# Splitting the 512-column matmuls of an expert layer's output product into two of 256 columns

## The chip, the cores and the metric

The kernel runs on one NeuronCore of a Trainium2 chip. The metric is the device time of one execution in microseconds (us). Durations of single instructions are given in nanoseconds (ns).

## The reference

Three layers follow one another; the change lies in the third. The tokens are N = 2304, the model width is 512.

```python
# 1. attention with keys and values averaged over groups of 8 (4 batches, 8 heads, 576 x 64)
# 2. gated layer: (sigmoid(x @ w_gate) * (x @ w_val)) @ w_out, width 1536
# 3. eight experts, width 1024 each, all of them for every token:
P = np.exp(logits - logits.max())              # logits = x @ w_gate, [N, 8]
for _ in range(8):                             # rows and columns normalised in turn
    P /= P.sum(1, keepdims=True) + 1e-09
    P /= P.sum(0, keepdims=True) + 1e-09
    P *= N / E
for e in range(E):
    h = np.maximum(x @ w1[e], 0.0)             # first product
    ye = h @ w2[e]                             # second product: the one that is changed
    out += P[:, e:e+1] * ye
```

## The kernel before, in words

All large products take fp32 data split into a high and a low part of the type fp32r, and multiply in three passes (high with high, high with low, low with high: `PASSES`, L260). Every `nc.tensor.matmul` becomes two instructions on TensorE: a weight load (LDWEIGHTS, the `lhsT` operand, 128 rows by up to 128 columns) and a MATMUL, which streams the columns of `rhs` past those weights into a bank of PSUM. The trace keeps the loads on a row of their own (PEld). Consecutive matmuls never share a load, even where they use the same `lhsT` (the first two passes do).

The attention and the gated layer take the first third of the time. Their large products are made by `mm` (L262, matmuls at L268) and `x2_step` (L506, matmuls at L560), all with 384 streamed columns. Attention has small matmuls of plain fp32, such as the scores at L351 (64 rows of weights, 72 columns).

The expert layer works through 96 steps (`steps2`: 3 pairs of token blocks, 8 experts, 4 parts of the expert's width; the loop begins at L973). A pair holds two blocks of 384 tokens. In each step:

- The first product is made by seven block products (`product`, L895, matmuls at L903), six matmuls of 384 columns each, with sums and differences of blocks as operands (prepared by GpSimd and ScalarE in `prep_w1`, L697 to L708). Their results go through ScalarE copies (L1011, L1019, L1026), VectorE additions (L1032, L1038, L1045) and `hidden` (L913), which applies the ReLU and splits the result into the tiles `h`, two buffers each.
- The second product of the step before is made by `y_chunk` (L922), called six times, once for every 128 tokens. Each call takes a bank of 512 fp32 from the tag "big" (four buffers), runs six matmuls of 512 columns into it (two halves of the width `fh`, three passes each; `lhsT` is a 128-column slice of `h`, `rhs` a row of `w2hl`, the split weights of `prep_w2`, L716 and L717), and hands the bank to VectorE, which multiplies by the token's share `prob` and adds to `acc` in one instruction (L963).

The order of TensorE's work is the order in which the loop writes it: a product, then a `y_chunk`, and so on, so that the engines that finish a product have the following six matmuls' time for it. After the last step six calls of `y_chunk` follow with nothing between them (L1057), and the results leave by DMA from `acc` (L967). The change touches only the six matmuls of `y_chunk`, L929 to L937: 3456 matmuls in all (96 steps, 6 calls, 6 each).

Of the kernel before, what the change touches and what calls it, by code (L numbers as in the profile page):

```python
# [20 lines left out]
def attention_moe_moe_kernel(  # L21
# [31 lines left out]
    nc = tc.nc  # L53
    NT, DM = out.shape
# [30 lines left out]
    def bank(tag, bufs):  # L85
        return ps.tile([128, 512], F32, tag=tag, name=tag, bufs=bufs)
# [173 lines left out]
    PASSES = ((0, 0), (0, 1), (1, 0))  # L260
# [406 lines left out]
    raw1, raw2, wsum, w2hl = {}, {}, {}, {}  # L667
# [59 lines left out]
    with tc.manual_schedule():  # L727
# [151 lines left out]
        hs = {}  # L879
# [42 lines left out]
        def y_chunk(n, t):  # L922

            if n < 0:
                return
            p, e, q = steps2[n]
            half, i = divmod(t, TPB)
            cs = slice(i * 128, (i + 1) * 128)
            py = bank("big", 4)  # L929
            m = 0  # L930
            for fh in range(2):
                h = hs[n, fh, half]
                for s, o in PASSES:
                    nc.tensor.matmul(  # L934
                        out=py, lhsT=h[:, s, cs], rhs=w2hl[n][:, o, fh], start=(m == 0), stop=(m == 5)
                    )
                    m += 1  # L937
            tt = p * CPP + t
            pr = prob[:, tt, e : e + 1]
            if p == 0 and e < LATE:  # L940
                if q == 0:
                    raw_acc[e, t] = pools["more"].tile([128, DM], F32, tag="acc", name="acc", bufs=LATE * CPP)
                    nc.scalar.copy(out=raw_acc[e, t], in_=py)
                else:
                    nc.vector.tensor_tensor(out=raw_acc[e, t], in0=py, in1=raw_acc[e, t], op=ALU.add)
                return
            if e == 0 and q == 0:
                acc[t] = pools["more"].tile([128, DM], F32, tag="acc", name="acc", bufs=LATE * CPP)
                nc.vector.tensor_scalar_mul(out=acc[t], in0=py, scalar1=pr)
            else:  # L950
                if p == 0 and t not in acc:
                    acc[t] = raw_acc[0, t]
                    nc.scalar.activation(out=acc[t], in_=acc[t], func=AF.Copy, scale=prob[:, tt, 0:1])
                    for i in range(1, LATE):
                        nc.vector.scalar_tensor_tensor(
                            out=acc[t],
                            in0=raw_acc[i, t],
                            scalar=prob[:, tt, i : i + 1],
                            in1=acc[t],
                            op0=ALU.mult,  # L960
                            op1=ALU.add,
                        )
                nc.vector.scalar_tensor_tensor(  # L963
                    out=acc[t], in0=py, scalar=pr, in1=acc[t], op0=ALU.mult, op1=ALU.add
                )
            if (e, q) == (E - 1, QF - 1):
                nc.sync.dma_start(out=out[tt * 128 : (tt + 1) * 128], in_=acc[t])  # L967
# [5 lines left out]
        for n, (p, e, q) in enumerate(steps2):  # L973
# [38 lines left out]
            if last_of_pair:  # L1012
                load_xf(p + 1, 0)
            y_chunk(n - 1, 3)
            slot2()
            if n > 0:
# [3 lines left out]
            if last_of_pair:  # L1020
                load_xf(p + 1, 3)
            y_chunk(n - 1, 4)
            slot2()
            product(n, "P6", pa, False)
            c2 = c_tile()
            nc.scalar.copy(out=c2, in_=pa[:, :TB])  # L1026
            if last_of_pair:
                load_xf(p + 1, 4)
            y_chunk(n - 1, 5)
            slot2()  # L1030
            product(n, "P3", pc, False)
# [86 lines left out]
```

## Time and profile before

| What | Value |
|---|---|
| Time, median of 2 runs | 2180.82 us (2176.22 and 2185.43) |
| Span of the profiled execution, first to last instruction | 2185.2 us |
| The run's time that stands beside that span | 2185.43 us |
| TensorE matmul, busy | 2096.2 us (96%), 10973 instructions |
| TensorE weight load, busy | 1905.0 us (87%), 10973 instructions |
| VectorE, ScalarE, GpSimd, busy | 65%, 40%, 41% |
| Matmuls of the changed line, L934 | 3456, recorded 394 ns each |

The span belongs to one execution; the run nearest to it took 0.2 us more. A matmul's record is longer than the time until the next matmul starts, because matmuls follow one another in a pipeline and the recorded end is modelled. The distance from one start to the next ("pitch" below) therefore tells more than the recorded length. The records of weight loads likewise may overlap one another.

### The profile page before, as it was taken

To read this page: it belongs to the slowest core of one execution; us is meant where nothing else is said; L and a number is where in the kernel's file an instruction comes from. 1 tells how busy PE (TensorE), PEld (TensorE's weight loads), DVE (VectorE), ACT (ScalarE), POOL (GpSimd) and SP (SyncE) were. 2 spreads that over 40 slices of the span, in tenths; PEclk is the share of its full clock that TensorE was granted. 3 is DMA by queue.
4 is the path that set the end of the run, shared out by engine and by line. 5 is a ranking of instruction groups with operands and counts; after the bars stand their busy time and mean duration, and the time that the engine had idled before them with its cause. 6 is when DMAs were issued, how large, how long until landed. Compare 5 with 4: busy or idle time off the path is not lost.

```text
span 2185.2 us, 28656 instructions
## 1 busy us (share of the span) xinstructions
PE 2096.2 (96%) x10973; PEld 1905.0 (87%) x10973; DVE 1422.6 (65%) x2172; ACT 882.5 (40%) x1607; POOL 891.5 (41%) x780
## 2 busy tenths in 40 slices
PE   4679999999999999999999999999999999999999
PEld 4568989988997888888888898989888888898988
DVE  6846876644435877666666666666666666666665
ACT  4334343454544444434343434343433343434342
POOL 1100000353554465454545454545454545454541
PEclk8679999999999999999999999999999999999999
DMA  7432553453562132121215121212125212121211
GB/s 227 143 119 85 167 171 116 131 181 106 194 228 92 59 116 78 61 75 60 76 59 206 58 78 58 78 58 78 58 78 188 77 58 78 58 78 58 78 58 39
DMA packets 87451, 222.09 MB, mean 102 GB/s; under 512 B 8849, under 2 KB 8849, under 8 KB 87313
## 3 DMA queue, kind: packets, MB, share of 16 engines
q1 hardware_dynamic: 82128, 210.81, 28.5%
q10 hardware_dynamic: 5184, 9.44, 1.2%
q8 instruction: 86, 1.41, 0.3%
q14 instruction: 53, 0.43, 0.1%
HBM read 189.55 MB, written 30.67 MB: 101 GB/s over the span
## 4 chain that ended last, share of the span: by engine, by line
PE 86%; DVE 6%; issue 3%; ACT 2%; DMA 1%; POOL 1%; SPq 0%; ACTq 0%; DVEq 0%; POOLq 0%
PE big L934 37%; PE at L903 18%; PE gv L903 14%; PE gv L268 10%; PE big L560 4%; DVE wa_lo L236 1%; PE at L351 1%; DMA narrow<-made 1%; PE at L437 1%; DVE made L166 1%; DVE made L165 1%; DVE g L821 1%; ACT wa_hi L231 1%; PE at L422 0%; DVE wide L175 0%
## 5 line engine op out<-in xcount | busy, mean ns | idle before, releaser
L934 PE MATMUL big<-w2hl,h 128*128 128x512 f32 x3456 | 893.8, 394 | 0.0
L934 PEld LDWEIGHTS big<-w2hl,h 128*128 128x128 f32 x3456 | 642.0, 188 | 102.2
L963 DVE SCALAR_TENSOR_TENSOR acc<-big,prob,acc 128x512 f32<-128x512 f32 x516 | 385.6, 748 | 264.8 <-PE big L934 258.7
L705 POOL TENSOR_TENSOR fa<-raw,fa 128x768 fp32r<-128x768 f32 x96 | 179.4, 1869 | 440.0 <-PE big L934 403.2
L268 PE MATMUL gv<-xs,wa_hi 128*128 128x384 f32 x1152 | 314.6, 355 | 20.9 <-ACT xs L447 8.1
L707 POOL TENSOR_TENSOR fs<-ss,fs 128x512 fp32r<-128x512 f32 x96 | 125.0, 1303 | 292.9 <-ACT fs L704 289.3
L268 PEld LDWEIGHTS gv<-xs,wa_hi 128*128 128x128 f32 x1152 | 217.1, 198 | 28.2 <-ACT xs L447 8.9
L917 ACT ACTIVATE h<-gv 128x384 fp32r<-128x384 f32 x192 | 94.3, 491 | 355.2 <-DVE gv L1045 196.4
L903 PE MATMUL at<-xf,fa 128*128 128x384 f32 x1152 | 233.7, 338 | 0.8 <-DVE c L1038 0.8
L903 PE MATMUL at<-xf,fs 128*128 128x384 f32 x1152 | 232.4, 337 | 0.4 <-ACT c L1011 0.4
L903 PE MATMUL gv<-xf,fs 128*128 128x384 f32 x1152 | 231.6, 336 | 0.0
L717 DVE TENSOR_TENSOR w2hl<-raw,w2hl 128x512 fp32r<-128x512 f32 x192 | 227.6, 1186 | 6.1 <-ACT w2hl L716 6.1
L903 PEld LDWEIGHTS at<-xf,fa 128*128 128x128 f32 x1152 | 206.6, 189 | 17.7 <-DVE c L1038 1.6
L903 PEld LDWEIGHTS gv<-xf,fs 128*128 128x128 f32 x1152 | 205.4, 188 | 16.3
L268 PE MATMUL gv<-xs,wa_lo 128*128 128x384 f32 x576 | 203.1, 353 | 14.8 <-DVE wa_lo L236 11.8
L903 PEld LDWEIGHTS at<-xf,fs 128*128 128x128 f32 x1152 | 204.4, 188 | 9.0 <-ACT c L1011 0.7
L918 DVE SCALAR_TENSOR_TENSOR h<-gv,h 128x384 fp32r<-128x384 f32 x192 | 107.2, 558 | 107.6 <-ACT h L917 107.6
L560 PE MATMUL big<-h,wa_hi 128*128 128x384 f32 x576 | 150.8, 343 | 0.0
L594 POOL TENSOR_TENSOR fx<-x,fx 128x768 fp32r<-128x768 f32 x10 | 18.4, 1844 | 316.5 <-DVE x L577 263.4
L236 POOL TENSOR_TENSOR wa_lo<-stage,wa_hi 128x512 fp32r<-128x512 f32 x67 | 99.6, 1499 | 81.3 <-ACT wa_hi L231 69.6
L268 PEld LDWEIGHTS gv<-xs,wa_lo 128*128 128x128 f32 x576 | 114.7, 199 | 17.7 <-DVE wa_lo L236 14.6
L708 POOL TENSOR_TENSOR fs<-ss,fs 128x512 fp32r<-128x512 f32 x96 | 125.5, 1307 | 0.0
(149 smaller groups left out, 2682.1 us busy)
## 6 DMA issues: line engine op xcount, KB each, us to landing
raw<-in_moe_w_dram SPq DMA_DIRECT2D x192, 512.0 KB, 3.8
stage<-narrow SPq DMA_DIRECT2D x150, 256.0 KB, 2.8
xd<-fx SPq DMA_DIRECT2D x21, 768.0 KB, 3.3
xf<-xd SPq DMA_DIRECT2D x21, 768.0 KB, 6.6
narrow<-made ACTq DMA_DIRECT2D x36, 256.0 KB, 2.0
wide<-in_moe_w_gate_dram SPq DMA_DIRECT2D x12, 512.0 KB, 3.8
wide<-in_moe_w_val_dram SPq DMA_DIRECT2D x12, 512.0 KB, 10.0
wide<-in_moe_w_out_dram SPq DMA_DIRECT2D x12, 512.0 KB
```

The lines of the kernel that those rows point to most:

```text
L236: eng.tensor_tensor(out=lo, in0=raw, in1=f32(hi), op=ALU.subtract)
L268: nc.tensor.matmul(out=out_, lhsT=a[s], rhs=b[m], start=(i == 0), stop=(i == n - 1))
L560: nc.tensor.matmul(out=x2p[d][:, :TB], lhsT=w[s][:, d * 128 : (d + 1) * 128], rhs=gs[j, f][m], start=(first and i == 0), stop=(last and i ...
L705: pl(out=fa[:, 1], in0=raw[:, 0:3], in1=f32(fa[:, 0]), op=ALU.subtract)
L707: pl(out=fs[:, 1, 0:2], in0=ss[:, 0:2], in1=f32(fs[:, 0, 0:2]), op=ALU.subtract)
L708: pl(out=fs[:, 1, 2:4], in0=ss[:, 2:4], in1=f32(fs[:, 0, 2:4]), op=ALU.subtract)
L717: nc.vector.tensor_sub(out=t[:, 1, i], in0=raw[:, i], in1=f32(t[:, 0, i]))
L903: nc.tensor.matmul(out=pt[:, :TB], lhsT=w[:, s, i, k], rhs=t[:, o, k], start=(start and m == 0), stop=(m == 5), skip_group_check=True,)
L917: nc.scalar.activation(out=t[:, 0], in_=src, func=AF.Relu)
L918: nc.vector.scalar_tensor_tensor(out=t[:, 1], in0=src, scalar=0.0, in1=f32(t[:, 0]), op0=ALU.max, op1=ALU.subtract)
L934: nc.tensor.matmul(out=py, lhsT=h[:, s, cs], rhs=w2hl[n][:, o, fh], start=(m == 0), stop=(m == 5))
L963: nc.vector.scalar_tensor_tensor(out=acc[t], in0=py, scalar=pr, in1=acc[t], op0=ALU.mult, op1=ALU.add)
```

## The change

In `y_chunk`, the six matmuls of 512 columns become two groups of six with 256 columns each: first all six for columns 0 to 255 of the bank, then all six for columns 256 to 511. Each of the twelve has a weight load of its own, so the same `lhsT` slice is loaded twice as often. The bank, its buffers and what follows on VectorE stay as they are.

```diff
             py = bank("big", 4)
-            m = 0
-            for fh in range(2):
-                h = hs[n, fh, half]
-                for s, o in PASSES:
-                    nc.tensor.matmul(
-                        out=py, lhsT=h[:, s, cs], rhs=w2hl[n][:, o, fh], start=(m == 0), stop=(m == 5)
-                    )
-                    m += 1
+            for d0 in range(0, DM, 256):
+                m = 0
+                for fh in range(2):
+                    h = hs[n, fh, half]
+                    for s, o in PASSES:
+                        nc.tensor.matmul(
+                            out=py[:, d0 : d0 + 256],
+                            lhsT=h[:, s, cs],
+                            rhs=w2hl[n][:, o, fh, d0 : d0 + 256],
+                            start=(m == 0),
+                            stop=(m == 5),
+                        )
+                        m += 1
             tt = p * CPP + t
```

## Rows read from the trace of the kernel before

**Rows 1.** The page: busy time by engine, and the chain by line.

```profile
PE 2096.2 (96%) x10973; PEld 1905.0 (87%) x10973; DVE 1422.6 (65%) x2172; ACT 882.5 (40%) x1607; POOL 891.5 (41%) x780
...
PE big L934 37%; PE at L903 18%; PE gv L903 14%; PE gv L268 10%; PE big L560 4%; DVE wa_lo L236 1%; PE at L351 1%; DMA narrow<-made 1%; PE at L437 1%; DVE made L166 1%; DVE made L165 1%; DVE g L821 1%; ACT wa_hi L231 1%; PE at L422 0%; DVE wide L175 0%
```

**Rows 2.** Busy time by stretch (us): the expert layer, 682 to 2181.

```profile
682.00:2181.00 1499.00, 1498.18 (x7460) 1345.50 (x7458) 1015.18 (x1501) 599.64 (x1067) 721.62 (x658) 1.00 0.23 78
```

**Rows 3.** Waits of TensorE between 690 and 2181 us (total, times, longest).

```profile
PE at L903 <- DVE c L1038: 0.8, 1, 0.8
```

**Rows 4.** Groups of instructions, shapes apart: busy us, mean ns of one; idle before.

```profile
L934 PE MATMUL big<-w2hl,h 128*128 128x512 f32 x3456 | 893.8, 394 | 0.0
L934 PEld LDWEIGHTS big<-w2hl,h 128*128 128x128 f32 x3456 | 642.0, 188 | 102.2
...
L903 PEld LDWEIGHTS at<-xf,fa 128*128 128x128 f32 x1152 | 206.6, 189 | 17.7 <-DVE c L1038 1.6
```

**Rows 5.** Timeline of TensorE's matmuls from 1500 us: start, length of the run, count.

```profile
1500.65 1.55 PE L934 MATMUL big<-w2hl,h 128*128 128x512 f32 x6
1502.04 1.21 PE L903 MATMUL gv<-xf,fs 128*128 128x384 f32 x6
1503.09 1.55 PE L934 MATMUL big<-w2hl,h 128*128 128x512 f32 x6
1504.48 1.22 PE L903 MATMUL at<-xf,fs 128*128 128x384 f32 x6
1505.53 1.55 PE L934 MATMUL big<-w2hl,h 128*128 128x512 f32 x6
1506.92 1.21 PE L903 MATMUL gv<-xf,fs 128*128 128x384 f32 x6
1507.96 1.20 PE L903 MATMUL at<-xf,fs 128*128 128x384 f32 x6
1509.00 1.55 PE L934 MATMUL big<-w2hl,h 128*128 128x512 f32 x6
```

**Rows 6.** Timeline of the weight loads, same stretch.

```profile
1500.48 1.29 PEld L934 LDWEIGHTS big<-w2hl,h 128*128 128x128 f32 x6
1501.81 1.12 PEld L903 LDWEIGHTS gv<-xf,fs 128*128 128x128 f32 x6
```

**Rows 7.** Timeline of VectorE at the end, one instruction per `y_chunk`.

```profile
2177.29 0.75 DVE L963 SCALAR_TENSOR_TENSOR acc<-big,prob,acc 128x512 f32<-128x512 f32 x1 [0.61 <-PE big L934]
2178.65 0.75 DVE L963 SCALAR_TENSOR_TENSOR acc<-big,prob,acc 128x512 f32<-128x512 f32 x1 [0.61 <-PE big L934]
2180.01 0.75 DVE L963 SCALAR_TENSOR_TENSOR acc<-big,prob,acc 128x512 f32<-128x512 f32 x1 [0.61 <-PE big L934]
```

**Rows 8.** Timeline of the weight loads around the scores, from 262 us.

```profile
262.26 0.96 PEld L351 LDWEIGHTS at<-kp,qt 64*128 64x128 f32 x8 [0.25 <-PE gv L268]
263.30 0.30 PEld L560 LDWEIGHTS big<-h,wa_hi 128*128 128x128 f32 x2
```

**Rows 9.** Timeline of the matmuls around the scores, from 262 us.

```profile
263.30 0.62 PE L560 MATMUL big<-h,wa_hi 128*128 128x384 f32 x2
```

**Rows 10.** Timeline of matmuls with weights of 8 columns, from 366 us.

```profile
366.24 0.52 PE L268 MATMUL at<-fx,wg_hi 128*8 128x384 f32 x2
366.59 0.34 PE L268 MATMUL at<-fx,wg_lo 128*8 128x384 f32 x1
366.77 0.51 PE L268 MATMUL at<-fx,wg_hi 128*8 128x384 f32 x2
```

**Rows 11.** Busy time by stretch: 160.4 to 162 us, granted clock 0.50 (third figure from the end).

```profile
160.40:162.00 1.60, 1.60 (x6) 1.60 (x6) 0.00 (x0) 0.30 (x1) 0.00 (x0) 0.50 0.92 292
```

**Rows 12.** Timeline of the matmuls in that stretch.

```profile
160.83 0.84 PE L268 MATMUL gv<-xs,wa_hi 128*128 128x384 f32 x2
161.47 0.52 PE L268 MATMUL gv<-xs,wa_lo 128*128 128x384 f32 x1
161.79 0.84 PE L268 MATMUL gv<-xs,wa_hi 128*128 128x384 f32 x2
162.44 0.52 PE L268 MATMUL gv<-xs,wa_lo 128*128 128x384 f32 x1
```

**Rows 13.** The page: DMA queues (packets, MB, share); q8 carries 16 KB packets of instructions.

```profile
q8 instruction: 86, 1.41, 0.3%
```

## The prediction

> **What bounds the kernel now.** I read the page first. TensorE's matmuls are busy for 96% of the span, and the chain that ended last runs through them: 37% of it is the changed line L934 and 32% the products at L903 [rows 1]. The reader should distrust the 96%, since the ends of matmuls are modelled, and look for idle time instead. The view by stretches says that between 682 and 2181 us, the whole expert layer, TensorE was busy for 1498.18 of 1499.00 us at a granted clock of 1.00, which is the higher level, 2.4 GHz [rows 2]. The waits of that stretch have one row, 0.8 us [rows 3]. So this layer lasts exactly as long as its matmuls take one after another. No other engine and no transfer ends last anywhere in it. What the change is worth is therefore the number of matmuls times the change in the distance from start to start, their pitch.
>
> The recorded length is not that pitch: 394 ns is the mean record at L934 [rows 4]. The pitch comes from the timeline. A run of six L934 matmuls starts at 1500.65 and the next run at 1502.04: 1.39 us for six. Three such runs give 4.17 us for 18, **231.7 ns for 512 columns**. The three runs at L903 that follow them take 1.05, 1.05 and 1.04 us, 3.14 us for 18, **174.4 ns for 384 columns** [rows 5]. Check: 3456 x 231.7 ns = 800.8 us, which is the 37% of the chain.
>
> **The change part by part.** It removes 3456 matmuls of 512 columns and adds 6912 of 256 columns. Columns streamed, operands, banks and the work of VectorE stay the same. What is added is 3456 further pairs of weight load and matmul start. Two costs are unknown, because no fp32r matmul under 384 columns stands in this trace: the pitch of the 256-column matmul by its own columns, and the pitch that its weight load forces.
>
> *By its columns.* A straight line through the two pitches has a slope of (231.7 - 174.4)/128 = 0.448 ns per column and meets zero columns at 2.5 ns. At 256 columns it gives 117.1 ns, almost half of 231.7. By this reading two halves cost 234.2 ns, 2.5 ns more than the whole. A less friendly reading comes from runs of one kind only. At the very end `y_chunk` follows `y_chunk`, and VectorE's instruction for each starts every 1.36 us, so six matmuls of 512 columns take 1360 ns, 226.7 each [rows 7]. Where a product follows a product, six of 384 take 1.04 us, 173.3 each (from 1506.92 to 1507.96 and on to 1509.00 [rows 5]). That line has a slope of 53.4/128 = 0.417 and meets zero at 13 ns: a fixed charge for every matmul. It gives 120.0 ns at 256 columns. Against a fixed charge speaks the stretch at half clock (0.50, the lower level of 1.2 GHz [rows 11]): there five starts span 162.44 - 160.83 = 1.61 us for five matmuls, 322 ns for 384 columns, and 384/1.2 is 320, so next to nothing is charged [rows 12]. I take **118 ns**, between 117.1 and 120.0 and nearer to the line that uses the same stretch.
>
> *By its load.* Each load is recorded with 188 ns, at L934 as at L903 [rows 4]. That is more than 118, so the reader must see whether loads can follow one another faster than their records. They do. At L903 the matmuls start every 174 ns with a 188 ns load each. The scores show it better: eight loads of 128 columns stand in 0.96 us, (960 - 188)/7 = 110 ns from load to load, with matmuls of only 72 columns between them [rows 8]. The two loads of L560 that follow cover 0.30 us, so the second began 0.11 us after the first [rows 8]. These loads are fp32r, and 0.11 us is what a load holds its place for. Does a load hide beneath the matmul before it? The first two matmuls there cover 0.62 us; the second one's record being about 0.34 us (a row of [rows 10] has that length for 384 columns), it began 0.28 us after the first, which is 0.11 of unhidden load plus one pitch of 0.17 [rows 9]. All later ones run at 0.174, so each load is hidden. And loads of 8 columns give no faster stream: 366.24 to 366.77 is 0.53 us for three matmuls, 177 ns [rows 10]. The load costs nothing as long as it fits: 110 ns fit beneath 117 to 120, with 7 to 10 ns to spare. That is the thin point of this forecast. For the load term I take 0 ns; its bounds are -11.7 ns per old matmul (pitch falls to the load's 110: 2 x 110 - 231.7) and, with nothing hidden, 2 x 110 more than the columns cost.
>
> The Trainium skill bears on this cover. "TensorE: Matmul & The Clock Gate", Part 3, under what overlaps and what doesn't, says that a weight load overlaps matmuls in flight only if it is aimed at other row groups of the array. Here every load takes all 128 rows, so by that rule each half would cost 117 + 110 = 227 ns and the kernel 3456 x (454 - 231.7) = 768 us more. The trace disagrees: a load of 110 ns and 384 columns, 160 ns at 2.4 GHz, would need 270 ns one after another, and the row shows 174.
>
> *The rest.* TensorE gets 6912 more instructions, and one of the instruction queues, q8, brought 86 packets of 16 KB; 1.41 MB over TensorE's 21,946 instructions is 64 bytes each, so I take it for TensorE's queue [rows 1, 13]. Some 27 more will come, in the expert layer one every 17.5 us instead of 26 (255 instructions a packet, and 21,830 instead of 14,918 in 1499 us [rows 2]). Cost: nothing now, as TensorE waits once in 1491 us [rows 3]; if every added packet stalled it for the time that one takes (0.3% of 16 x 2185 us over 86: 1.2 us), 33 us. I take 0. VectorE waits for the last matmul of a chunk as before and holds the bank for 0.75 of 1.36 us [rows 7]; the banks come free as before.
>
> *Sum.* 3456 x (2 x 118 - 231.7) ns = 3456 x 4.3 ns = +14.9 us. On the profiled execution that is 2185.4 + 14.9 = 2200.3 us. Its time lies 4.6 us above the median of the two runs, so on the median's scale I predict 2180.8 + 14.9 = **2195.7 us**: 0.7% more, less than the 2% that a measurement of this kernel can tell from no change. Each ns of the new pitch is worth 6.9 us, and 2% is 43.6 us: the pitch would have to pass 122.3 ns to be slower, or fall under 109.4 to be faster.
>
> **The rivals.**
>
> *The weight load takes over (slower).* The load of a matmul begins only when the matmul before has started: the two load runs start at 1500.48 and 1501.81, each about 0.17 to 0.23 us ahead of their first matmul, that is with the start of the one before [rows 5, 6]. If the loop of load, hand-over and next start is longer than 118 ns, it sets the pitch. Its length lies between 110 [rows 8] and 174 (it fits into L903's pitch); it decides from 122.3. If it needed the whole record and a start, 190 ns, the price would be 3456 x (380 - 231.7) = +512 us, but L903 excludes that. At 174, the longest that the rows allow, it is 3456 x 116.3 = +402 us, 2583; at 140 it is +167 us. For it: the loads would be in their place 110 of 118 ns, which no fp32r stream here has had to stand; the nearest, L903, has 110 of 174. Against it: the scores hold 110 with loads alone.
>
> The Trainium skill has a rule that leads to this side: "Perfetto Trace Analysis", on identifying the most-contended engine, wants TensorE's headroom judged by the busy share of its weight loads. That share is 87% now; 3456 more of 188 ns (650 us) would make 2555 us in a span of 2185, so the time would have to grow by hundreds of us. The rows of the scores speak against it, where 188 ns records start 110 ns apart.
>
> *A fixed charge of 13 ns per matmul (no change that can be told).* The pitch is 120.0, the price 3456 x 8.3 = +29 us, 2209.5. For it the pure runs, against it the half clock.
>
> *The halves run faster than half.* If what slows the long streams (231.7 for 512 columns, where 512/2.4 is 213.3) is absent in short ones, the load alone bounds the pitch at 110: 3456 x -11.7 = -40 us, 2140. For it: 226.7 at the end shows that the pitch isn't rigid. Against it: nothing in the rows gets shorter than its share of columns.
>
> *The loads are shared, so nothing is added.* Consecutive matmuls with the same `lhsT` have a load each today (10973 and 10973 [rows 1]), so the change does what it says.
>
> **How the numbers follow.** Pitch of 114 to 122.3, the forecast with the fixed charge: 0.68 (0.50 and 0.18). Load takes over, above 122.3: 0.23. Faster halves, under 114: 0.09, of which about half falls under 109.4. So faster by over 2%: 0.05; within 2%: 0.72; slower: 0.23. The range begins at 2150 (pitch 111.4, nearly the load's 110) and ends at 2250 (pitch 125.9), which takes in the first part of the load rival; about 0.04 lies below and 0.15 above.
>
> **What would show it.** In the profile after, a chunk of twelve matmuls should take 1.40 to 1.44 us before the next product starts, L934's successors should stand with 6912 matmuls of about 280 ns record (394 less 256 columns of 0.448), L903 should keep its 1.04 to 1.05 us, and TensorE's waits in the layer should stay near nothing, with the granted clock at 1.00. If the load takes over, twelve take over 1.47 us. If all L934 chunks agree but gaps of a us or more appear every 17 us or so, it is the instruction queue. I am wrong if a chunk of twelve leaves 1.33 to 1.47 us.

## The result, and the profile after

The changed kernel takes **2210.58 us** (median; 2209.08 and 2212.08) against 2180.82 before: a ratio of 1.0133, with an interval of 1.0104 to 1.0161. That is 23 to 35 us more, slower by less than 2%, and the interval excludes no change. The prediction was 2195.7 us within 2150 to 2250.

The page of the kernel after begins with the busy times by engine; its part on DMA queues has the packets of instructions.

```profile
PE 2120.2 (96%) x14429; PEld 2078.1 (94%) x14429; DVE 1420.5 (64%) x2172; ACT 883.0 (40%) x1607; POOL 891.6 (40%) x780
...
q8 instruction: 113, 1.85, 0.4%
...
L935 PE MATMUL big<-w2hl,h 128*128 128x256 f32 x6912 | 918.1, 283 | 0.0
L935 PEld LDWEIGHTS big<-w2hl,h 128*128 128x128 f32 x6912 | 898.6, 191 | 0.0
```

Against [rows 1] and [rows 4]: 3456 more matmuls and as many more loads, so no load was shared. The other engines' busy times are those of before. The view by stretches shows the expert layer and, last in its row, the clock and the DMA share:

```profile
682.00:2203.00 1521.00, 1520.27 (x10902) 1519.92 (x10901) 1013.36 (x1501) 599.54 (x1066) 721.33 (x658) 1.00 0.22 77
```

As in [rows 2], matmuls fill the stretch at a clock of 1.00. What is new is the second figure: loads now fill it too (1519.92 of 1521.00 us; 1345.50 of 1499.00 before). The waits of TensorE in the layer are still one row:

```profile
PE at L903 <- DVE c L1043: 0.7, 1, 0.7
```

So the time has not gone into a wait. It is in the pitch, the distance from start to start. Timeline of the matmuls from 1500 us (start, length, count):

```profile
1500.42 1.59 PE L935 MATMUL big<-w2hl,h 128*128 128x256 f32 x12
1501.85 1.20 PE L903 MATMUL gv<-xf,fs 128*128 128x384 f32 x6
1502.89 1.21 PE L903 MATMUL at<-xf,fs 128*128 128x384 f32 x6
1503.94 1.59 PE L935 MATMUL big<-w2hl,h 128*128 128x256 f32 x12
1505.37 1.20 PE L903 MATMUL gv<-xf,fa 128*128 128x384 f32 x6
1506.41 1.59 PE L935 MATMUL big<-w2hl,h 128*128 128x256 f32 x12
1507.84 1.21 PE L903 MATMUL at<-xf,fa 128*128 128x384 f32 x6
1508.88 1.60 PE L935 MATMUL big<-w2hl,h 128*128 128x256 f32 x12
1510.32 1.21 PE L903 MATMUL at<-xf,fa 128*128 128x384 f32 x6
```

Four chunks of twelve take 1.43, 1.43, 1.43 and 1.44 us, 5.73 us for 48: **119.4 ns a half**. Over all 569 chunks that stand between products the mean is 1.435 us, 119.6 ns a half. A chunk was 1.39 us [rows 5]. The products at L903 keep their 1.04 to 1.05 us. Now the sum: 3456 x (2 x 119.4 - 231.7) = +24.5 us. The starts of the line's first and last matmul give the same: 682.1 to 2180.9 us before and 680.0 to 2203.1 after, 1498.8 and 1523.2 us when not rounded first, +24.4. This stretch is called the layer's time below. The profiled spans differ by 22.1, as the first two layers happened to take 2 us less in the second one.

Timeline of VectorE at the end of the kernel after, where chunk follows chunk:

```profile
2199.14 0.75 DVE L968 SCALAR_TENSOR_TENSOR acc<-big,prob,acc 128x512 f32<-128x512 f32 x1 [0.69 <-PE big L935]
2200.59 0.75 DVE L968 SCALAR_TENSOR_TENSOR acc<-big,prob,acc 128x512 f32<-128x512 f32 x1 [0.69 <-PE big L935]
2202.03 0.75 DVE L968 SCALAR_TENSOR_TENSOR acc<-big,prob,acc 128x512 f32<-128x512 f32 x1 [0.69 <-PE big L935]
2203.46 0.75 DVE L968 SCALAR_TENSOR_TENSOR acc<-big,prob,acc 128x512 f32<-128x512 f32 x1 [0.69 <-PE big L935]
```

4.32 us for three chunks, 1.44 each: 120.0 ns a half, against 226.7 for a whole matmul in the same place [rows 7]. In such a uniform stream the halves cost 13.3 ns more than the whole; between products, where the whole takes 231.7, they cost 7.1.

### The profile page after: what moved, and what is told of

It reads as the page before. It is cut to its first block, busy times and chain, and to the rows that moved or that the text cites. A ratio compares the mean times of both kernels' runs of the same rounds, so it can differ in the third digit from the quotient of the medians.

```text
span 2207.3 us, 35657 instructions
## 1 busy us (share of the span) xinstructions
PE 2120.2 (96%) x14429; PEld 2078.1 (94%) x14429; DVE 1420.5 (64%) x2172; ACT 883.0 (40%) x1607; POOL 891.6 (40%) x780
## 4 chain that ended last, share of the span: by engine, by line
PE 87%; DVE 6%; issue 2%; ACT 2%; DMA 2%; POOL 0%; SPq 0%; ACTq 0%; DVEq 0%; POOLq 0%
PE big L935 37%; PE at L903 18%; PE gv L903 14%; PE gv L268 10%; PE big L560 5%; DVE wa_lo L236 1%; PE at L351 1%; DMA narrow<-made 1%; PE at L437 1%; DVE made L166 1%; PE at L422 1%; DMA wide<-in_moe_w_gate_dram 1%; DVE wide L175 1%; DVE g L821 0%; ACT wa_hi L231 0%
## 5 line engine op out<-in xcount | busy, mean ns | idle before, releaser
L935 PE MATMUL big<-w2hl,h 128*128 128x256 f32 x6912 | 918.1, 283 | 0.0
L935 PEld LDWEIGHTS big<-w2hl,h 128*128 128x128 f32 x6912 | 898.6, 191 | 0.0
L903 PE MATMUL at<-xf,fa 128*128 128x384 f32 x1152 | 233.5, 337 | 0.7 <-DVE c L1043 0.7
L903 PE MATMUL gv<-xf,fs 128*128 128x384 f32 x1152 | 233.2, 337 | 0.0
L903 PE MATMUL at<-xf,fs 128*128 128x384 f32 x1152 | 232.1, 336 | 0.4 <-ACT c L1016 0.4
L717 DVE TENSOR_TENSOR w2hl<-raw,w2hl 128x512 fp32r<-128x512 f32 x192 | 223.1, 1163 | 6.4 <-ACT w2hl L716 6.4
L903 PEld LDWEIGHTS at<-xf,fs 128*128 128x128 f32 x1152 | 197.6, 188 | 0.8 <-ACT c L1016 0.7
L903 PEld LDWEIGHTS at<-xf,fa 128*128 128x128 f32 x1152 | 193.9, 189 | 0.9 <-DVE c L1043 0.9
L903 PEld LDWEIGHTS gv<-xf,fs 128*128 128x128 f32 x1152 | 194.0, 190 | 0.2 <-issue 0.2
```

Of the source, the lines that this page charges most:

```text
L717: nc.vector.tensor_sub(out=t[:, 1, i], in0=raw[:, i], in1=f32(t[:, 0, i]))
L903: nc.tensor.matmul(out=pt[:, :TB], lhsT=w[:, s, i, k], rhs=t[:, o, k], start=(start and m == 0), stop=(m == 5), skip_group_check=True,)
L935: nc.tensor.matmul(out=py[:, d0 : d0 + 256], lhsT=h[:, s, cs], rhs=w2hl[n][:, o, fh, d0 : d0 + 256], start=(m == 0), stop=(m == 5),)
```

## Experiments

### Does the load set the pitch? Quarters, and an uneven split

Two readings gave about 119.5 ns: F, a fixed charge of 13 ns on every matmul with the load hidden, and L, the load with its hand-over taking over. Quarters of 128 columns leave the load no cover, so it shows its own pitch:

```diff
-            for d0 in range(0, DM, 256):
+            for d0 in range(0, DM, 128):
...
```

(The slices of 256 columns become slices of 128.)

> Four matmuls of 128 columns in place of each 512: the columns ask for 53 ns, so the load must set the pitch and shows its own. F: 110 to 112 ns, as at the scores, so 4 x 111 - 231.7 = +212 ns for each of 3456, about 2915 us. L: 119.5 ns, +246 ns each, about 3032 us. Above 125 ns: neither; then short fp32r streams cost something of their own.

Measured: 2920.39 us in a single run, as F expects. Timeline of VectorE at the end:

```profile
2906.75 0.75 DVE L968 SCALAR_TENSOR_TENSOR acc<-big,prob,acc 128x512 f32<-128x512 f32 x1 [1.93 <-PE big L935]
2909.43 0.75 DVE L968 SCALAR_TENSOR_TENSOR acc<-big,prob,acc 128x512 f32<-128x512 f32 x1 [1.93 <-PE big L935]
```

2.68 us for 24 matmuls, 111.7 ns: that is what a load of 128 columns holds its place for, as at the scores [rows 8], and not 119.5. The Trainium skill's page "TensorE: Matmul & The Clock Gate", in its section on LDWEIGHTS, gives a load's time as its columns over 1.2 GHz, which makes an estimate of 107 ns for 128; this run agrees within 5 ns.

The uneven split is at 288:

```diff
-            for d0 in range(0, DM, 256):
+            for d0, d1 in ((0, 288), (288, DM)):
...
```

> The split at column 288 instead of 256: 288 and 224 columns. F: 288/2.4 + 13.3 = 133 ns, 224/2.4 + 13.3 = 107 ns, raised to the load's 110 to 112 ns: a pair of 243 to 245 ns against 239 in the changed kernel, 2224 to 2231 us. L: 133 + 119.5 = 252.8 ns a pair, 13.8 ns more than in the changed kernel, 2258 us.

Measured: 2223.82 us, ratio 1.0203 (1.0181 to 1.0225). Timeline of its matmuls:

```profile
1500.92 1.62 PE L935 MATMUL big<-w2hl,h 128*128 128x288 f32 x12
1502.38 1.23 PE L903 MATMUL gv<-xf,fs 128*128 128x384 f32 x6
1503.44 1.61 PE L935 MATMUL big<-w2hl,h 128*128 128x288 f32 x12
1504.89 1.23 PE L903 MATMUL at<-xf,fs 128*128 128x384 f32 x6
```

1.46 and 1.45 us for six pairs, 242.5 ns a pair (a row of the timeline names the first of the two shapes only). The starts one by one give 129 to 133 ns for 288 columns; for 224 the first of six takes 103 and the others 111 to 114. L's 119.5 for the shorter one is gone. Streams of 224 and of 128 columns have nearly the same pitch, some 111 to 112 ns, which speaks for the load setting it in both. It does not take over at 256.

### Is it the adding into the same columns? The halves inside the passes

```diff
-            for d0 in range(0, DM, 256):
-                m = 0
-                for fh in range(2):
-                    h = hs[n, fh, half]
-                    for s, o in PASSES:
+            m = 0
+            for fh in range(2):
+                h = hs[n, fh, half]
+                for s, o in PASSES:
+                    for d0 in range(0, DM, 256):
```

> The changed kernel, but with the two halves inside the passes: each lhsT slice is used twice in a row, and successive matmuls write different halves of the bank. F and L: no difference, 2210 us within 4, pitch 119.5. Rival A (the charge comes from adding into the columns that the matmul before has just written): the pitch falls towards 107 to 116 ns, the time to 2140 to 2186 us.

Measured: 2205.23 us, ratio 1.0112 (1.0094 to 1.0131). The starts one by one give 119.5 ns on average, and the layer took 1522.6 us against 1523.2 in the changed kernel, so the lower time comes from what stands ahead of the layer. Rival A falls: neither the column range written before nor a load of the very same weights matters. In this kernel the first pass of the first half is left out of the sum; its sister moves the start mark and keeps the pass:

```diff
-                            start=(m == 0),
+                            start=(m == 0 and d0 == 0),
```

> The two halves inside the passes as before, but only the very first matmul of a bank carries the start mark; the second half's first matmul doesn't. In the earlier kernel of this kind the second half's start, coming behind the first half's first pass in the same bank, wiped that pass, so it was left out of the sum. All theories of the time: pitch 119 to 120 ns, 2205 to 2210 us.

Measured: 2204.19 us in a single run, and 119.5 ns.

### How much of the charge is the load? Lighter loads

```diff
+                    w = 128 - 64 * fh
...
-                            out=py[:, d0 : d0 + 256],
-                            lhsT=h[:, s, cs],
+                            out=py[:w, d0 : d0 + 256],
+                            lhsT=h[:, s, i * 128 : i * 128 + w],
...
```

(In this kernel and the next ones the stop marks change with it, so that the rows which the light matmuls no longer write are closed by the last full one.)

> The changed kernel, but the last three matmuls of each six (second half of the width) load only 64 weight columns and write 64 rows: half of that contribution is left out. Theory F (every fp32r matmul pays about 13 ns on top of its columns at 2.4 GHz, the load of 110 ns is hidden): those 3456 matmuls keep a pitch of 118 to 120 ns, time as in the changed kernel, 2210 us within 4. Rival L (the load with its hand-over sets the pitch of 119.5): a load of half the columns takes about 55 ns less, so the columns set the pitch of these matmuls, 107 to 116 ns, and the time falls by 3456 x 4 to 12 ns, to 2170 to 2196 us.

Measured: 2194.78 us, ratio 1.0072 (1.0051 to 1.0093), at the upper end of what L expected and outside F. So F is not the whole story either. Timeline:

```profile
1501.84 1.57 PE L936 MATMUL big<-w2hl,h 128*128 128x256 f32 x12
1503.24 1.23 PE L903 MATMUL at<-xf,fs 128*128 128x384 f32 x6
```

This chunk takes 1.40 us instead of 1.43; the mean over the layer is 1.414. The next kernel has `w = 128 - 112 * fh`, 16 weight columns in three of six:

> The changed kernel, but the last three matmuls of each six load 16 weight columns and write 16 rows; seven eighths of that contribution are left out. C with a cost in proportion to the load's columns: 119.5 less 6 ns, 113 to 114 ns, 3456 x -6 = -20 us against the changed kernel, 2188 us. T, or a charge that any narrower load avoids: as with 64 columns, 116 ns, 2195 us. A charge with no part of the load in it would have shown no difference at 64 columns.

Measured: 2191.93 us, ratio 1.0043 (1.0026 to 1.0059), between the two expectations. Its chunk is 1.40 us as well, 1.407 in the mean:

```profile
1502.68 1.56 PE L936 MATMUL big<-w2hl,h 128*128 128x256 f32 x12
1504.08 1.22 PE L903 MATMUL at<-xf,fs 128*128 128x384 f32 x6
```

Then five of six, with only the first load full:

```diff
...
+                        w = 16 if m else 128
...
```

> The changed kernel, but five of each six matmuls load 16 weight columns and write 16 rows (seven eighths of their contribution are left out); only the first loads 128. Theory G (half or more of the 13 ns charge belongs to a full load beside a 256-column stream): four of six follow narrow by narrow at 113 ns or less, a chunk of twelve takes 1.37 to 1.39 us at the end against 1.44, the time falls by some 25 to 35 us against the changed kernel, 2175 to 2185 at a before of 2180. Rival N (the earlier gain came from changing the load's width, not from its size): 120 ns between narrow ones, 1.42 us or more, 2200 us or more.

Measured: 2195.39 us, ratio 1.0053 (1.0037 to 1.0070). The time lies between G and N, and neither is right: the chunk is 1.40 us again, 1.405 in the mean.

```profile
1501.63 1.56 PE L936 MATMUL big<-w2hl,h 128*128 128x256 f32 x12
1503.03 1.22 PE L903 MATMUL at<-xf,fa 128*128 128x384 f32 x6
1504.09 1.56 PE L936 MATMUL big<-w2hl,h 128*128 128x256 f32 x12
1505.49 1.22 PE L903 MATMUL gv<-xf,fs 128*128 128x384 f32 x6
```

Three kernels with loads lightened by a quarter to nearly three quarters in all come to 117.8, 117.3 and 117.1 ns a half in the mean, against 119.6. So the gain is not in proportion to what the loads lost, and it stops near the 117.1 of the line through the mixed pitches [rows 5]. Single starts still lie between 113 and 121 ns apart. The products behind such chunks take 1.053 us instead of 1.048 in the mean, so part of the gain is given back there: of the 24.4 us that the layer had gained in length, the three kernels take back 8.8, 12.6 and 13.9.

These kernels change more than the weight of the loads. Neighbouring loads become unequal, and fewer rows of the bank are written. None of the three keeps one of these apart from the others.

The same at 512 columns, three of six with 64 weight columns:

> The kernel before (512 columns), but the last three matmuls of each six load 64 weight columns and write 64 rows; half of that contribution is left out. With halves of 256 columns, such loads took 3 to 4 ns off the pitch. Theory C (a load beside a stream slows that stream a little, whatever its length): the same 3 to 4 ns go here, 231.7 to about 228 for 1728 matmuls, -6 us, 2173. Theory T (the hand-over from load to matmul is what is too tight at 256 columns): with 232 ns of cover nothing changes, 2179 us within 3.

Measured: 2188.12 us, ratio 1.0028 (1.0014 to 1.0041): no gain, so C falls, and T, which had no change, missed the loss. It stands at the products behind such chunks, 1.059 us in the mean against 1.048. Timeline of VectorE at its end:

```profile
2178.71 0.75 DVE L970 SCALAR_TENSOR_TENSOR acc<-big,prob,acc 128x512 f32<-128x512 f32 x1 [0.62 <-PE big L936]
2180.08 0.75 DVE L970 SCALAR_TENSOR_TENSOR acc<-big,prob,acc 128x512 f32<-128x512 f32 x1 [0.62 <-PE big L936]
2181.45 0.75 DVE L970 SCALAR_TENSOR_TENSOR acc<-big,prob,acc 128x512 f32<-128x512 f32 x1 [0.62 <-PE big L936]
```

1.37 us where equal loads gave 1.36 [rows 7]. And five of six with 16:

> The same loads with 512 columns (five of six with 16 weight columns, the same part left out). If the load's share of the charge is there at any length: 1.33 us or less for a chunk at the end against 1.36, the time under that of before by 10 to 20 us. If it is there only where the load fills the matmul beside it: 1.36 us or a little more, 2180 us within 5 or slower.

Measured: 2179.26 us, ratio 0.9992 (0.9977 to 1.0007). A chunk at the end takes 1.39 us:

```profile
2171.17 0.75 DVE L970 SCALAR_TENSOR_TENSOR acc<-big,prob,acc 128x512 f32<-128x512 f32 x1 [0.64 <-PE big L936]
2172.55 0.75 DVE L970 SCALAR_TENSOR_TENSOR acc<-big,prob,acc 128x512 f32<-128x512 f32 x1 [0.64 <-PE big L936]
2173.95 0.75 DVE L970 SCALAR_TENSOR_TENSOR acc<-big,prob,acc 128x512 f32<-128x512 f32 x1 [0.64 <-PE big L936]
```

At 512 columns a load has 232 ns of cover, and making it lighter saves nothing in sum: between products the chunks take 1.391 and 1.385 us against 1.393, and the products behind them give that back. At the end of the kernel, where 512 columns took 226.7 ns, the unequal loads even cost time: five light ones of six bring back the 231.7 ns of the mixed stretch.

This leaves two readings of the few ns at 256 columns. One is that the load costs them because it fills 111 of the 120 ns beside it. The other is that unequal neighbours, whatever they weigh, put a stream on the line through the mixed pitches: that line has 117.1 ns for 256 columns and 231.7 for 512, and five light loads of six show 116.7 and 231.7 at the end of the kernel. The second reading needs no cost of the load at all. Nothing here decides between them, or rules out the rows that are not written.

### Where do the 5 ns between 226.7 and 231.7 come from? Chunks in a row

```diff
             load_xf(p + 1, 0)
-            y_chunk(n - 1, 3)
+            for t in (3, 4, 5):
+                y_chunk(n - 1, t)
...
-            y_chunk(n - 1, 0)
+            for t in (0, 1, 2):
+                y_chunk(n - 1, t)
```

(The four other calls in the step go away.)

> The kernel before with its 512-column matmuls, but three chunks in a row at two places of a step instead of six places with one. In the mixed stretch 512 columns take 231.7 ns, at the end, where chunks follow one another, 226.7 from some nine matmuls after the last product on. Theory M (the 5 ns come from alternating with the products): the third chunk and half of the second of each three run at 226.7, -45 ns x 2 x 96 = -9 us, 2170 us. Theory S (they come from what the other engines do): all stay at 231.7, 2179 us within 3. A new wait of TensorE for a product's result would add to either and would stand in its waits.

Measured: 2178.1 us, ratio 0.9981 (0.9968 to 0.9994). Timeline:

```profile
1505.72 4.30 PE L934 MATMUL big<-w2hl,h 128*128 128x512 f32 x18
1509.86 1.20 PE L903 MATMUL gv<-xf,fs 128*128 128x384 f32 x6
```

Eighteen take 4.14 us, 230.0 ns. One by one and averaged over the 190 such runs, the first six take 224 to 236 ns, the next three 229, 232 and 231, and from the tenth on every one takes 226.7 (only the last before a product 233). That is M: other engines work on beside all eighteen, so S falls. In the layer's time the chunks became 10.3 us cheaper, where M asked for 9. But the products, which now follow one another in longer rows, took 5.1 us more, so the saving is 0.2% and not M's 0.4%. It is the fastest of the versions that compute the whole sum.

If the split costs what the rows say, it must cost more in this order, where the whole matmul has lost part of its 5 ns:

> Both changes: the halves of 256 columns, and three chunks in a row at two places of a step. If the price of the split is the charge per matmul (halves 119.5 to 120.0 in any order) less the 5 ns that only the long matmuls pay when they alternate with products: against three in a row with 512 columns (229.4 ns) the halves cost 2 x 119.8 - 229.4 = 10.2 ns, 3456 times, +35 us, and against the kernel before +29 us, about 2211. If three in a row saves its 5 us whatever the width: 5 us less than the changed kernel, ratio to before 1.011, about 2205.

Measured: 2211.75 us, ratio 1.0145 (1.0124 to 1.0165): +32 us on its before of 2179.77, and 1.64% of 2180 or 36 us more than three in a row without the split. Expected were +29 and +35; the rival's 1.011 lies outside. In the layer's time it is 33.9 us between the two traces. Timeline:

```profile
1499.89 4.47 PE L935 MATMUL big<-w2hl,h 128*128 128x256 f32 x36
1504.20 1.20 PE L903 MATMUL gv<-xf,fs 128*128 128x384 f32 x6
```

4.31 us for 36, 119.7 ns; from the thirteenth on the starts are 120.0 apart.

All six chunks of 512 columns in a row, at the second of the two places:

> 512 columns, all six chunks in a row at one place of a step. If alternation alone costs the 5 ns, four and a half chunks of six run at 226.7: 135 ns x 96 = 13 us less than before, 2170 us at a before of 2183 (three in a row: 9 us expected, 5 to 6 found). If products that follow one another wait for copies between them, waits of TensorE at L903 appear and eat it: each us per step would be 96 us.

Measured: 2236.12 us, ratio 1.0256 (1.0242 to 1.0270), not the 13 us less that alternation alone would give: the waits that were feared have come. The 36 matmuls in a row did fall to 229.5 ns in the mean. Waits of TensorE, 690 to 2230 us, the three largest in sum:

```profile
PE gv L903 <- ACT c L1018: 17.0, 91, 0.9
PE big L934 <- DVE acc L945: 10.0, 5, 2.8
PE at L903 <- ACT c L1011: 2.5, 2, 2.0
```

With no chunk between them the products stand behind ScalarE's copies. Timeline of the matmuls of one step:

```profile
1504.87 1.20 PE L903 MATMUL at<-xf,fs 128*128 128x384 f32 x6
1506.25 1.31 PE L903 MATMUL gv<-xf,fs 128*128 128x384 f32 x6 [0.17 <-ACT c L1018]
1507.40 1.20 PE L903 MATMUL at<-xf,fs 128*128 128x384 f32 x6
```

A product that should take 1.04 us takes 1.38, and the next one 1.15. That is 0.45 us a step, 42 of the 47 us that the layer became longer; the row of waits shows only the part that lies behind the recorded end of a matmul. What M promises can be had for three in a row but not for six.

## Why the prediction was right or wrong

- **What bounds the layer: right.** Matmuls fill 1520.27 of 1521.00 us, the clock stayed at 1.00, TensorE waited 0.7 us in all, and the difference is 3456 times the difference in pitch, within 1 us of the trace. A chunk of twelve took 1.43 to 1.44 us, inside the 1.40 to 1.44 that were named as the sign.
- **The pitch of a half: this step failed.** The sum took 118 ns for the columns and 0 for the load; the rows after show 119.4, and 120.0 where halves follow one another. The 1.4 ns are, but for rounding, the 9.6 us between the 14.9 that were forecast and the 24.5 in the trace. The line through the uniform runs, 120.0, is exact for uniform halves, and the rival of a fixed charge that stands on it, +29 us and 2209.5, came out nearest to the median. It had been given 0.18. The row at half clock, which argued against it, did not carry over: there 384 columns take 322 ns where 384/1.2 is 320, at full clock 173.3 where 384/2.4 is 160.
- **"The load costs nothing as long as it fits": not settled.** The load does hide: its own pitch is 111.7 ns, and of the widths tried it sets the pitch only at 224 and 128 columns. Kernels with lighter loads have halves that are 1.8 to 2.5 ns faster, and a layer that is 9 to 14 of the 24.4 us shorter. The 0 may be wrong by that much; but unequal loads alone may do the same, as the runs at 512 columns suggest, so no run has shown this term by itself.
- **The load takes over (23%): did not happen**, as quarters and the uneven split show. The point from which it would decide was not reached. (That point, and the one for faster, are 122.2 and 109.5 ns, not 122.3 and 109.4: 43.6 us over 6912 halves is 6.3 ns on either side of 115.85.)
- **The faster halves: did not happen.** Even with light loads the average stops at 116.7.
- **The Trainium skill's rule that loads overlap only across row groups**, as the prediction quoted it, would have given 768 us more; the trace of the change disagrees as that of before did, with 119.4 ns where 227 were asked for. The busy share of loads did rise, to 94%, but adding 650 us of records added 173 us of busy time and 24 us of time: records overlap.
- **The instruction queue: right.** 113 packets, 27 more, and no wait.
- **The range tells little.** 2210.58 lies within 2150 to 2250, but so do the forecast, the fixed charge and the first part of the load rival. Only the pitch in the trace tells them apart, and by the medians the change costs 29.8 us, twice what was forecast.

Open is what the 13.3 ns of uniform streams are (226.7 for 512 columns, 173.3 for 384, 120.0 for 256: the columns over 2.4 GHz plus 13.3 each), and why an alternation of lengths or of load widths replaces them by 0.448 ns per column and 2.5 ns. Uniform halves with uniformly light loads were not tried, nor light loads that write all rows, so the 2 ns have no shown cause. The Trainium skill's page "TensorE: Matmul & The Clock Gate", section on the back-to-back issue gap, gives for the isolated gap the columns over 2.4 GHz plus 2.5 ns; for 256 and 512 columns that is an estimate of 109 and 216 ns. No stream of fp32r matmuls here came that near: the lowest means were 116.7 and 226.7.

## What to carry to other kernels

Where matmuls fill the time, price a split by starts and not by records: halves of 256 fp32r columns with a load of 128 weight columns each cost 7 ns more than the whole between other products and 13 ns more in a row, and at 224 and 128 columns the load of 111 ns set the pitch. Where two lines through the rows disagree, as 117.1 and 120.0 did here, do not settle it by a row at another clock. Whether a cover that is only a few per cent longer than what it hides costs something by itself is not shown. Calibrate the pitch in a stretch of the same mixture as the one that is changed, and put its load beside it.

## What was not expected of the hardware

Fp32r matmuls of 512 columns run at 226.7 ns among their own kind and at 231.7 after matmuls of another length, and the effect dies away nine matmuls after the last of these, while the other engines work on as before. Halves of 256 columns show no such surcharge (118 to 121 between products, 120.0 in a row). Loads of unequal width in a row move both lengths, and in opposite directions: from 226.7 to 231.7 ns at 512 columns, from 120.0 to 116.7 at 256. Streams of 128 columns, the shortest fp32r ones tried, have no cost of their own beyond the load (111.7 ns).
